# Using the second column half of one w_in block before its gate column exists, while the next block is still landing

## The chip, the cores and the metric

The kernel runs on one core of one Trainium2 chip. Times are device microseconds (us) of one execution. An execution is one sample; medians are given with their range and number. The effect looked for is about 0.1% of the time, smaller than the spread of single executions. Starts of instructions are in us from the start of the span.

## The reference, cut to what matters

The whole function mixes an attention branch and a gMLP branch with a gate. The part that is touched is the first product of the gMLP branch, and the gate's logit:

```python
z  = _gelu(jnp.einsum('bsd,df->bsf', x, w_in))     # x: 2048 x 512, w_in: 512 x 1376
z1 = z[..., :688]
z2 = _layernorm(z[..., 688:])
...
g  = _sigmoid((x * gate_w).sum(-1, keepdims=True)) # gate_w: 512
```

The kernel gets the logit almost for nothing: it stores gate_w as a 689th column beside the 688 columns of w_in that make z2.

## The kernel before

`w_z2` holds the z2 half of w_in in four blocks of 128 rows (the contraction, 512, in steps of 128). Each block has 688 columns from memory and the gate column at index 688. The columns are multiplied in two halves: half 0 is 344 columns, half 1 is 344 columns and the gate, 345. `xT` holds x transposed, in tiles of 128 rows of x.

```python
def z_one(zp, tt, wt, w, dt, j, first=0):          # one matmul: x tile tt, block dt, half j
    n = HF if j == 0 else w - HF                   # HF = 344
    nc.tensor.matmul(
        zp[:, j, 0:n], lhsT=xT[:, dt, tt * P:(tt + 1) * P],
        rhs=wt[:, dt, j * HF:j * HF + n],
        start=(dt == first), stop=(dt == NDT - 1),
    )

def gate_T():                                      # gate_w row -> column 688 of all four blocks
    gt = pq_tile([P, NDT])
    nc.tensor.matmul(gt[:, :], lhsT=gaterow[:, :], rhs=ident[:, 0:NDT], start=True, stop=True)
    nc.vector.tensor_copy(out=w_z2[:, :, FH], in_=gt[:, :])
```

The loads are issued so: half 0 of block 0, then blocks 1, 2 and 3 on one queue; two x tiles, half 1 of block 0, and the other x tiles on another; the gate row on a third. The first two x tiles are worked off in an order that follows the landings:

```python
def z2_first_two():
    # ... warm_up(n, w): n matmuls of constants, to get TensorE to its full clock;
    # ... one(tt, dt, j): z_one for x tile tt, with first=j
    warm_up(6); warm_up(2, P)
    # ... PE transposes of x tiles 0 and 1, mixed with one(0, 0, 0) and one(0, 1, 0) ...
    one(1, 0, 0)
    one(1, 1, 0)
    gate_T()
    one(0, 2, 0)                # block 2, half 0: here TensorE waits for block 2
    one(1, 2, 0)
    for dt in range(1, 3):      # blocks 1 and 2, half 1, with the gate column
        one(0, dt, 1)
        one(1, dt, 1)
    for tt in range(2):
        one(tt, 3, 0)
        one(tt, 0, 1)
        one(tt, 3, 1)
        z2_out(tt, zps[tt])
# then z2_tile(2), z2_tile(3), and so on: 8 matmuls each
```

The softmax here doesn't subtract the row's maximum and nothing guards it: scores larger than these inputs give would overflow.

Of the kernel before, what the change touches and what calls it, by code (L numbers as in the profile page):

```python
# [14 lines left out]
P = 128  # L15
# [6 lines left out]
HF = FH // 2  # L22
NT = S // P
NDT = D // P
# [11 lines left out]
def kernel(  # L36
# [14 lines left out]
    nc = tc.nc  # L51
# [10 lines left out]
    xT = pers.tile([P, NDT, S], BF16, name="xT")  # L62
    w_z1 = early.tile([P, NDT, FH], BF16, name="w_z1")
    w_z2 = early.tile([P, NDT, WP], BF16, name="w_z2")
# [111 lines left out]
    def next_turn(kind, n):  # L176
        turn[kind] += 1
        return f"{kind}{(turn[kind] - 1) % n}"

    def zp_tile():  # L180
        return psA.tile([P, 2, CH], FP32, name="zp", tag=next_turn("zp", 3))

    def pq_tile(shape, dtype=FP32):
        return psF.tile(shape, dtype, name="pq", tag=next_turn("pq", 2))

    def z_one(zp, tt, wt, w, dt, j, first=0):
        n = HF if j == 0 else w - HF
        nc.tensor.matmul(  # L188
            zp[:, j, 0:n], lhsT=xT[:, dt, tt * P:(tt + 1) * P],
            rhs=wt[:, dt, j * HF:j * HF + n],  # L190
            start=(dt == first), stop=(dt == NDT - 1),
        )

    def z_mm(tt, wt, w):
        zp = zp_tile()
        for dt in range(NDT):
            for j in range(2):
                z_one(zp, tt, wt, w, dt, j)
        return zp

    def z2_out(tt, zp):
        z2v = z2all[:, tt, :].rearrange("p (j n) -> p j n", j=2)
        nc.scalar.activation(out=z2v, in_=zp[:, :, 0:HF], func=AF.Gelu_apprx_tanh)  # L203
        nc.vector.tensor_copy(out=glog[:, tt:tt + 1], in_=zp[:, 1, HF:HF + 1])
        for j in range(2):
            nc.vector.bn_stats(out=bn6[:, tt, j, :], in_=z2v[:, j, :])  # L206
        nc.vector.bn_aggr(out=mv[:, tt, :], in_=bn6[:, tt, :, :].rearrange("p j s -> p (j s)"))
# [4 lines left out]
    def z2_first_two():  # L212
        zps = [zp_tile() for _ in range(2)]
        tp1 = psA.tile([P, 2, P], BF16, name="tp1", tag=next_turn("zp", 3))
        turn["zp"] -= 1

        def warm_up(n, w=CH):
            for _ in range(n):
                nc.tensor.matmul(
                    zps[0][:, 1, 0:w], lhsT=nc.const_aps.tensor(1.0, [P, P], BF16),  # L220
                    rhs=nc.const_aps.tensor(1.0, [P, w], BF16), start=True, stop=True)

        def one(tt, dt, j):
            z_one(zps[tt], tt, w_z2, FH + 1, dt, j, first=j)

        warm_up(6)
        warm_up(2, P)
        x_T(0, 0, 1, pq_tile([P, 1, P], BF16)[:, :, :])
        x_T(0, 1, NDT, pq_tile([P, 3, P], BF16)[:, :, :])
        warm_up(3, P)  # L230
        one(0, 0, 0)
        x_T(1, 0, 2, tp1[:, :, :])
        x_T(1, 2, NDT, pq_tile([P, 2, P], BF16)[:, :, :], on_act=True)
        one(0, 1, 0)
        warm_up(1, P)
        one(1, 0, 0)
        one(1, 1, 0)
        gate_T()
        one(0, 2, 0)
        one(1, 2, 0)  # L240
        for dt in range(1, 3):
            one(0, dt, 1)
            one(1, dt, 1)
        for tt in range(2):
            one(tt, 3, 0)
            one(tt, 0, 1)
            one(tt, 3, 1)
            z2_out(tt, zps[tt])
# [21 lines left out]
    def x_T(i, d0, d1, tp, on_act=False):  # L270
        for dt in range(d0, d1):
            nc.tensor.transpose(tp[:, dt - d0, :], xs[:, i, dt * P:(dt + 1) * P], ident[:, :])
        dst = xT[:, d0:d1, i * P:(i + 1) * P]
        if on_act:
            nc.scalar.copy(out=dst, in_=tp)
        else:
            with tc.high_priority():
                nc.vector.tensor_copy(out=dst, in_=tp)

    def gate_T():  # L280
# [3 lines that stand above are left out]
# [27 lines left out]
    with tc.manual_schedule(engines={mybir.EngineType.PE, mybir.EngineType.Activation}):  # L311
        z2_first_two()
        z2_tile(2)
        z2_tile(3)
        for c in range(NCH):
            ts = list(range(c * 4, c * 4 + 4))
            for tt in ts:
                if c > 0:
                    z2_tile(tt)
                if c >= 2 and tt % 4 == 1:  # L320
                    later = fold(3 - c)
            for tt in ts:
                z1_tile(tt)
                if c >= 2 and tt % 2 == 0:
                    later.pop(0)()
            z2_norm(ts)
            if c == 1:
                b_T()
# [268 lines left out]
```

## Time and profile before

| | before |
|---|---|
| time, median of 3 | 207.93 us (207.68 to 208.12) |
| span of the profiled execution | 206.3 us |
| TensorE (PE) busy | 202.2 us, 98% |
| TensorE waiting for block 2 | 0.2 us |

The busy table of the page, and the first line of its chain that ended last (shares of the span by engine):

```profile
PE 202.2 (98%) x1536; PEld 120.3 (58%) x1536; DVE 128.8 (62%) x276; ACT 76.5 (37%) x123; POOL 45.4 (22%) x73
...
PE 95%; DMA 2%; ACT 1%; ACTq 0%; DVE 0%; issue 0%
```

TensorE bounds the kernel. Its list of waits (us in total, times, longest) holds two entries in the whole execution:

```profile
PE zp L219 <- PEq L581: 0.8, 1, 0.8
PE zp L188 <- DMA w_z<-in_B_w_in_dram: 0.2, 1, 0.2
```

The second is the one in question. TensorE's timeline around it (start, duration, engine, line, instruction, count, in brackets the idle time before; the window asked for ends at 9.6 us). L188 is `z_one`, L219 the warm-up, L282 the matmul of `gate_T`:

```profile
5.32 0.31 PE L219 MATMUL zp<-const-bfloat16-1.0 128*128 128x128 bf16 x1
5.43 0.69 PE L188 MATMUL zp<-w_z,xT 128*128 128x344 bf16 x2
6.00 0.18 PE L282 MATMUL pq<-ident,gaterow 128*128 128x4 bf16 x1
6.41 3.38 PE L188 MATMUL zp<-w_z,xT 128*128 128x344 bf16 x22 [0.23 <-DMA w_z<-in_B_w_in_dram]
```

And the start of the chain in order of time: the load of block 2 lands at 1.74 + 4.62 us (6.37 before these are rounded), and the first matmul on it follows.

```profile
1.74 4.62 DMA w_z<-in_B_w_in_dram
6.37 0.04 issue
6.41 15.65 PE zp L188 x106
```

Two readings matter. First, one matmul's record is 0.31 us long, but matmuls overlap; what counts is the distance of their starts. For 344 columns that is 0.286 us before 5.90 us (as between the two of the second line) and 0.146 us after it: the clock doubled at 5.90 us in this execution. Second, TensorE really has room between about 6.0 and 6.4 us, more than the 0.23 us that the list shows, because the modelled end of the matmul before covers part of it.

The mark used from here on is the **stretch**: from the start of the first matmul on block 2 (6.409 us here) to the start of the first matmul of x tile 2 (8.163 us), 1.754 us. It is twelve matmuls, 12 x 0.146.

### The profile page before, as it was taken

The numbers are of one execution on the slowest core, as the hardware profiler recorded it, in microseconds if no ns is written. First come the engines' busy times: TensorE is split into PE (matmuls) and PEld (weight loads), VectorE is DVE, ScalarE is ACT, GpSimd is POOL, SyncE is SP. The second block draws the span as 40 slices with busy tenths as digits, with TensorE's granted clock in tenths as the row PEclk, the third lists the DMA queues.
The fourth block names the chain that finished last, engine by engine and source line by source line (L and its number), as shares of the span: only waits on it lengthen the run. The fifth ranks groups of instructions, "written<-read, shape, count | busy, mean of one in ns | idle before, by whom it ended". The sixth has DMA issues, their size and how long they took to land.

```text
span 206.3 us, 3946 instructions
## 1 busy us (share of the span) xinstructions
PE 202.2 (98%) x1536; PEld 120.3 (58%) x1536; DVE 128.8 (62%) x276; ACT 76.5 (37%) x123; POOL 45.4 (22%) x73
## 2 busy tenths in 40 slices
PE   8999999999999999999999999999999999999994
PEld 4566666655666555556565666555455555665642
DVE  3367565746977777979797778555466553633330
ACT  2756677796222243333424032222251126001322
POOL 5020202020522326244242422222204220200000
PEclk9999999999999999999999999999999999999999
DMA  6999499999998025940443229763554767353642
GB/s 169 268 199 182 91 235 210 253 210 248 208 290 147 3 38 131 322 93 15 88 28 64 51 38 117 144 115 73 105 153 89 79 104 190 58 104 70 129 91 78
DMA packets 90099, 27.22 MB, mean 132 GB/s; under 512 B 84224, under 2 KB 90080, under 8 KB 90080
## 3 DMA queue, kind: packets, MB, share of 16 engines
q1 hardware_dynamic: 87168, 24.28, 62.0%
q10 hardware_dynamic: 2880, 2.68, 4.1%
q8 instruction: 12, 0.20, 0.4%
q14 instruction: 7, 0.06, 0.1%
q0 software_dynamic: 32, 0.00, 0.0%
HBM read 4.15 MB, written 2.10 MB: 30 GB/s over the span
## 4 chain that ended last, share of the span: by engine, by line
PE 95%; DMA 2%; ACT 1%; ACTq 0%; DVE 0%; issue 0%
PE mm L441 36%; PE zp L188 17%; PE mm L346 14%; PE mm L480 8%; PE mm L478 7%; PE mm L386 7%; DMA w_z<-in_B_w_in_dram 2%; PE at L454 2%; PE kvacc L402 2%; PE mm L483 1%; PE zp L299 0%; ACT z1all L252 0%; ACT wq_p L306 0%; ACTq L117 0%; ACTq L120 0%; PE pq L299 0%
## 5 line engine op out<-in xcount | busy, mean ns | idle before, releaser
L441 PE MATMUL mm<-z2all,wspT 128*128 128x344 bf16 x512 | 79.9, 309 | 0.0
L441 PEld LDWEIGHTS <-wspT 128*128 128x128 bf16 x512 | 49.0, 98 | 25.7 <-issue 0.4
L188 PE MATMUL zp<-w_z,xT 128*128 128x344 bf16 (+1 forms) x256 | 38.9, 312 | 0.2 <-DMA w_z<-in_B_w_in_dram 0.2
L350 ACT ACTIVATE eq<-mm 128x512 bf16<-128x512 f32 x32 | 17.4, 594 | 51.3 <-PE mm L346 21.3
L354 DVE TENSOR_REDUCE zs<-eq 128x64 f32<-128x1024 bf16 x16 | 19.5, 1220 | 20.3 <-ACT eq L350 20.3
L188 PEld LDWEIGHTS <-xT 128*128 128x128 bf16 x256 | 24.9, 98 | 12.4 <-issue 0.3
L446 DVE SCALAR_TENSOR_TENSOR ucat<-mm,bT,z1all 128x344 bf16<-128x344 f32 x32 | 17.4, 544 | 21.9 <-PE mm L441 21.9
L363 POOL TENSOR_TENSOR eq<-eq,ratio 128x512 bf16<-128x512 bf16 x16 | 16.9, 1059 | 49.9 <-DVE ratio L362 41.7
L350 ACT ACTIVATE ek<-mm 128x512 bf16<-128x512 f32 x32 | 17.3, 600 | 27.4 <-PE mm L346 27.4
L494 ACT ACTIVATE ob<-mm,g_inv 128x512 bf16<-128x512 f32 (+1 forms) x16 | 10.9, 681 | 32.8 <-PE mm L483 28.3
L354 DVE TENSOR_REDUCE zs<-ek 128x64 f32<-128x1024 bf16 x16 | 19.3, 1210 | 2.8 <-ACT ek L350 2.8
L480 PE MATMUL mm<-wspT,uT 128*128 128x512 bf16 (+2 forms) x85 | 20.1, 366 | 0.0
L346 PEld LDWEIGHTS <-xT 128*128 128x128 bf16 x128 | 12.2, 98 | 13.2 <-PE mm L483 0.8
L363 POOL TENSOR_TENSOR ek<-ek,ratio 128x512 bf16<-128x512 bf16 x16 | 17.0, 1059 | 2.1 <-DVE ratio L362 1.5
L478 PE MATMUL mm<-wspT,oT 128*128 128x512 bf16 (+2 forms) x68 | 16.6, 366 | 0.0
L346 PE MATMUL mm<-wq_p,xT 128*128 128x512 bf16 x64 | 16.4, 379 | 0.0
L386 PE MATMUL mm<-wv_sb,xT 128*128 128x512 bf16 x64 | 16.4, 379 | 0.0
L346 PE MATMUL mm<-wk_p,xT 128*128 128x512 bf16 x64 | 16.3, 379 | 0.1
L206 DVE BATCH_NORM_STATS2 bn<-z2all 128x6 f32<-128x344 bf16 x32 | 14.9, 503 | 0.0
L203 ACT ACTIVATE z2all<-zp 128x688 bf16<-128x688 f32 x16 | 11.8, 744 | 6.3 <-PE zp L188 6.3
L252 ACT ACTIVATE z1all<-zp 128x688 bf16<-128x688 f32 x16 | 11.9, 744 | 5.1 <-PE zp L188 4.6
L480 PEld LDWEIGHTS <-uT 128*128 128x128 bf16 x85 | 8.1, 98 | 9.2
(72 smaller groups left out, 142.7 us busy)
## 6 DMA issues: line engine op xcount, KB each, us to landing
out_dram<-ob ACTq DMA_DIRECT2D x15, 128.0 KB, 1.7
wspT<-in_B_w_out_dram SPq DMA_DIRECT2D x2, 640.0 KB, 5.2
w_z<-in_B_w_in_dram SPq DMA_DIRECT2D x2, 344.0 KB, 5.2
w_z<-in_B_w_in_dram ACTq DMA_DIRECT2D x3, 172.0 KB, 4.6
wv_sb<-in_A_wqkv_dram SPq DMA_DIRECT2D x2, 256.0 KB, 3.5
wspT<-in_A_wo_dram SPq DMA_DIRECT2D x2, 256.0 KB, 3.9
xs<-in_A_x_dram SPq DMA_DIRECT2D x2, 128.0 KB, 2.7
uT<-ucat SPq DMA_TRANSPOSE x16, 2.8
```

The costliest lines, as they stand in the source:

```text
L188: nc.tensor.matmul(zp[:, j, 0:n], lhsT=xT[:, dt, tt * P:(tt + 1) * P], rhs=wt[:, dt, j * HF:j * HF + n], start=(dt == first), stop=(dt == ...
L206: nc.vector.bn_stats(out=bn6[:, tt, j, :], in_=z2v[:, j, :])
L252: nc.scalar.activation(out=z1all[:, tt, :].rearrange("p (j n) -> p j n", j=2), in_=zp[:, :, 0:HF], func=AF.Gelu_apprx_tanh,)
L346: nc.tensor.matmul(ps[:, :], lhsT=xT[:, dt, tt * P:(tt + 1) * P], rhs=w[:, dt, :], start=(dt == 0), stop=(dt == NDT - 1))
L350: nc.scalar.activation(out=e[:, :, a, :], in_=ps[:, :].rearrange("p (h f) -> p h f", f=DH), func=AF.Exp, scale=1.0 - 2.0 * a)
L354: nc.vector.tensor_reduce(out=z[:].rearrange("p h a -> p (h a)"), in_=e[:].rearrange("p h a f -> p (h a) f"), axis=AX.X, op=ALU.add,)
L363: nc.gpsimd.tensor_tensor(out=e[:, :, 1, :], in0=e[:, :, 1, :], in1=ratio[:, :, None].to_broadcast([P, H, DH]), op=ALU.mult)
L386: nc.tensor.matmul(v_ps[:, :], lhsT=xT[:, dt, tt * P:(tt + 1) * P], rhs=wv_sb[:, dt, :], start=(dt == 0), stop=(dt == NDT - 1))
L441: nc.tensor.matmul(gp[:, 0:HF], lhsT=wspT[:, st, tt * P:(tt + 1) * P], rhs=z2all[:, st, j * HF:(j + 1) * HF], start=(st == 0), stop=(st == ...
L446: nc.vector.scalar_tensor_tensor(out=ucat[tt % NU][:, c0 + j * HF:c0 + (j + 1) * HF], in0=gp[:, 0:HF], scalar=bT[:, tt:tt + 1], in1=z1all[ ...
L478: nc.tensor.matmul(acc, lhsT=oT[:, g, :], rhs=wo_t[:, g, c0:c1], start=(g == 0), stop=False)
L480: nc.tensor.matmul(acc, lhsT=uT[:, i + ft, :], rhs=w_main[i][:, ft, c0:c1], start=False, stop=False)
```

## The change

Half 1 of block 1 landed at 4.34 us, well before block 2. It is not used there because its last column is the gate, which comes from `gate_T`. The change uses its 344 weight columns at once, in the wait, and adds the gate column of that block later, by two matmuls of one column.

```diff
-            start=(dt == first), stop=(dt == NDT - 1),
+            start=(dt == first), stop=(dt == NDT - 1), skip_group_check=first > 0,
@@
+        def z_part(tt, dt, c0, c1, start):
+            nc.tensor.matmul(
+                zps[tt][:, 1, c0:c1], lhsT=xT[:, dt, tt * P:(tt + 1) * P],
+                rhs=w_z2[:, dt, HF + c0:HF + c1], start=start, stop=False, skip_group_check=True)
@@
         one(1, 0, 0)
         one(1, 1, 0)
+        for tt in range(2):
+            z_part(tt, 1, 0, HF, True)
         gate_T()
         one(0, 2, 0)
         one(1, 2, 0)
-        for dt in range(1, 3):
-            one(0, dt, 1)
-            one(1, dt, 1)
+        for tt in range(2):
+            one(tt, 2, 1)
+            z_part(tt, 1, HF, HF + 1, False)
```

Why the gate column may be written first by `one(tt, 2, 1)`, which does not set `start`: the Trainium skill, "PSUM — Partial Sum Buffer" (The four PSUM rules), says that a matmul with the start flag clears the written-bits of the whole 2 KiB bank, and that a later one without the flag overwrites where the bit is clear. The argument `skip_group_check` belongs to the language that the kernel is written in.

## The prediction

> **What bounds the kernel now.** TensorE: busy 202.2 of 206.3 us (busy table), 95% of the chain of waits. Its list of waits holds two entries: 0.8 us at the start, and 0.2 us for a block of w_in. The change aims at the second. In the timeline the last matmuls before it start at 5.43 and 5.71 us, the gate transpose (gate_T) at 6.00 (its row landed at 5.95), the next matmul at 6.41, because block 2 of w_in lands at 6.37. From there TensorE streams: 94 matmuls of 344 or 345 columns in 13.9 us, starts 146 ns apart.
>
> **What the change does.** The second column half of block 1 (landed at 4.34) needs the gate only in its last column. The other 344 columns are now multiplied before gate_T, and the gate column later by two one-column matmuls.
> - Out of the stream after 6.41: two 345-column matmuls, 292 ns.
> - Into it: two one-column matmuls with weight loads. The trace has none; the 128x68 matmuls of kvacc, each with its weight load, start 30 ns apart. The Trainium skill ("TensorE: Matmul & The Clock Gate", Back-to-back issue gap) gives about 25 ns as floor for 1 to 64 columns. Estimate 28 each, 56 in sum.
> - Into the wait: two 344-column matmuls. Matmuls of 344 columns start 286 ns apart before about 5.90 and 146 after: the clock doubles there. So these start at about 5.95 and 6.10, gate_T at about 6.24, and TensorE is free by 6.28, before block 2.
>
> Expected gain: 292 - 56 = about 0.24 us, all on the critical path: no later wait in TensorE's list can swallow it.
>
> **What can eat part of it.** Three margins shrink to nearly nothing:
> 1. The gate column's copy on VectorE starts 0.21 us after gate_T and takes 0.18: it ends at about 6.64 (now 6.39); its first reader comes at about 6.70.
> 2. Block 3 lands at 7.01 and is first read at 7.29 now; then at about 7.05.
> 3. x tiles 2 and 3 land at 7.88 and are first read at 8.16 now; then at about 7.93.
> So with these landings the gain cannot exceed about 0.24 us, and later landings cut it. Where the clock doubles later (the same page, on the clock gate, says its window runs free of the kernel's start), the two early matmuls take 286 ns each and gate_T goes past 6.41; I estimate a gain of 0.1 to 0.3 then. I expect 0.2 on the mean.
>
> **Predicted time.** 207.93 - 0.21 = 207.72 us, range 207.4 to 208.0. Three runs of before spread over 0.44 us, twice the gain. Chances: faster by over 2% 0.003, within 2% 0.994, slower 0.003.
>
> **What would show each step right or wrong.**
> - TensorE's timeline: two more 344-column matmuls between 5.7 and 6.3, gate_T at about 6.25, the wait for block 2 nearly gone, the first block-2 matmul still at about 6.41.
> - The one-column matmuls at about 6.85 and 7.02, each followed by the next within 30 ns. If they cost 60 to 100 each, the gain halves.
> - Block 3's first matmul at about 7.05, at most a short new wait; x tile 2's first at about 7.93.
> - The rest shifted by about 0.2 us.
>
> **What would make it wrong.** The gate copy becoming what is waited for; weight loads that do not hide behind a one-column matmul; block 3 or the x tiles landing as the next limit.

## The result, and the profile after

| | before | after |
|---|---|---|
| median | 208.00 us (207.68 to 208.12, 4 runs) | 207.72 us (207.41 to 208.26, 4 runs) |
| ratio | | 0.9992, interval 0.9967 to 1.0016 |
| first matmul on block 2 | 6.409 us | 6.558 us |
| first matmul of x tile 2 | 8.163 us | 8.068 us |
| stretch | 1.754 us | 1.510 us |
| span | 206.26 us | 206.14 us |

Ratios are the mean time of one kernel's fast runs over that of the other's of the same rounds, so not quite the ratio of the medians. The interval includes 1 by a wide margin: the times alone show no difference. The outputs are right.

The page after, busy table and chain. TensorE's busy time should not be compared: this trace has 1538 weight loads but 1520 matmul records, so 18 are missing.

```profile
PE 200.9 (97%) x1520; PEld 120.3 (58%) x1538; DVE 128.8 (62%) x276; ACT 76.5 (37%) x123; POOL 45.4 (22%) x73
...
PE 94%; DMA 2%; ACT 1%; issue 1%; ACTq 0%; DVE 0%
```

TensorE's waits after, the same two entries:

```profile
PE zp L219 <- PEq L588: 0.8, 1, 0.8
PE zp L188 <- DMA w_z<-in_B_w_in_dram: 0.4, 1, 0.4
```

TensorE's timeline after. L227 is `z_part`, L289 the matmul of `gate_T`:

```profile
5.41 0.47 PE L188 MATMUL zp<-w_z,xT 128*128 128x344 bf16 x2
5.71 0.46 PE L227 MATMUL zp<-w_z,xT 128*128 128x344 bf16 x2
6.00 0.17 PE L289 MATMUL pq<-ident,gaterow 128*128 128x4 bf16 x1
6.56 0.60 PE L188 MATMUL zp<-w_z,xT 128*128 128x344 bf16 x3 [0.39 <-DMA w_z<-in_B_w_in_dram]
6.99 0.17 PE L227 MATMUL zp<-w_z,xT 128*128 128x1 bf16 x1
7.02 0.31 PE L188 MATMUL zp<-w_z,xT 128*128 128x345 bf16 x1
7.17 0.16 PE L227 MATMUL zp<-w_z,xT 128*128 128x1 bf16 x1
7.19 2.65 PE L188 MATMUL zp<-w_z,xT 128*128 128x344 bf16 x17
```

The chain, where block 2 lands at 1.75 + 4.77 = 6.52 us:

```profile
1.75 4.77 DMA w_z<-in_B_w_in_dram
6.52 0.04 issue
6.56 0.60 PE zp L188 x3
```

The two early matmuls stand at 5.71 and 5.86 us. The one-column matmuls start at 6.994 and 7.167 us, and the next matmuls 27 and 26 ns behind them. The stretch is 0.244 us shorter, as worked out beforehand. But block 2 landed 0.148 us later in this execution, and the clock had doubled a whole us earlier (at 4.90 us). So only 0.095 us of the gain is left at x tile 2, and those 0.1 us then travel through the whole execution: TensorE's last matmul starts at 203.20 us before and 203.10 after.

Two questions remain. Was the later landing a cost of the change, or chance? And does every execution gain 0.244 us in the stretch?

### The profile page after: what moved, and what is told of

It is laid out like the page before. It is cut to its first block, busy times and chain, and to the rows that moved or that the text cites. A ratio compares the mean times of both kernels' runs of the same rounds, so it can differ in the third digit from the quotient of the medians.

```text
span 206.1 us, 3932 instructions
## 1 busy us (share of the span) xinstructions
PE 200.9 (97%) x1520; PEld 120.3 (58%) x1538; DVE 128.8 (62%) x276; ACT 76.5 (37%) x123; POOL 45.4 (22%) x73
## 4 chain that ended last, share of the span: by engine, by line
PE 94%; DMA 2%; ACT 1%; issue 1%; ACTq 0%; DVE 0%
PE mm L448 36%; PE zp L188 17%; PE mm L353 13%; PE mm L487 8%; PE mm L393 7%; PE mm L485 7%; DMA w_z<-in_B_w_in_dram 2%; PE at L461 2%; PE kvacc L409 2%; PE mm L490 1%; PE zp L306 0%; ACT z1all L259 0%; ACT wq_p L313 0%; ACTq L117 0%; ACTq L120 0%
## 5 line engine op out<-in xcount | busy, mean ns | idle before, releaser
L188 PE MATMUL zp<-w_z,xT 128*128 128x344 bf16 (+1 forms) x254 | 38.4, 310 | 0.5 <-DMA w_z<-in_B_w_in_dram 0.4
L485 PE MATMUL mm<-wspT,oT 128*128 128x512 bf16 (+2 forms) x62 | 15.6, 365 | 0.3
```

The costliest lines, as they stand in the source:

```text
L188: nc.tensor.matmul(zp[:, j, 0:n], lhsT=xT[:, dt, tt * P:(tt + 1) * P], rhs=wt[:, dt, j * HF:j * HF + n], start=(dt == first), stop=(dt == ...
L485: nc.tensor.matmul(acc, lhsT=oT[:, g, :], rhs=wo_t[:, g, c0:c1], start=(g == 0), stop=False)
```

## The experiments

The theory at first: the gain is TensorE work moved out of the stretch (two matmuls out, two of one column in), the landing is chance. Rivals: the change makes block 2 land later; or a landing, not TensorE's work, sets the length of the stretch; or the stretch is shorter for another reason than the filled wait.

### The kernel before, again (no edit)

> The kernel before, unchanged, timed against itself: it shows how far five rounds differ by chance. Every theory expects 1.000, within 0.15%. Its trace gives a second look at the same program: the stretch from the first matmul of block 2 to the first matmul of x tile 2 should again be 1.75 us (1.754 in the first trace), whatever block 2's landing; block 2 should land between 6.3 and 6.6 us.

Measured: 208.01 us (207.33 to 208.48, 6 runs) against itself, ratio 1.0008, interval 0.9993 to 1.0023. Five rounds (repeated executions of both) thus cannot tell 0.1%. Stretch 1.754 us, with block 2 landing at 6.58 us.

### The changed kernel, again (no edit)

> The changed kernel, unchanged. My theory (two 345-column matmuls leave the stretch behind block 2 and two one-column matmuls of 27 ns come in) expects that stretch to be 1.51 us again, 0.24 us below the kernel before, and a time 0.1 to 0.3 us lower: ratio 0.9985 to 0.9995. Rival: block 2 landed 0.15 us later in the first trace of the changed kernel because of the change, so that the gain is partly paid back there; then it lands at 6.5 or later again, while the repeat of the kernel before lands at 6.4 or earlier. Rival: the landing is chance; then the two repeats show no such order.

Measured: 208.00 us (207.50 to 208.51, 6 runs), ratio 1.0010, interval 0.9996 to 1.0024, on the same chip and rounds as the run above; the expected 0.9985 to 0.9995 lies below this interval, but the kernel before against itself gave 1.0008 in these rounds. Block 2 landed at 5.84 us, much earlier than in the two traces of the kernel before up to then, so the rival that the change delays it has no support. The stretch missed the expectation: 1.654 us, not 1.51. These are three lines of the timeline of all engines around it (CAST on DVE is the copy of the gate column into w_z2):

```profile
6.03 0.74 PE L188 MATMUL zp<-w_z,xT 128*128 128x344 bf16 x3
6.18 0.10 PEld L188 LDWEIGHTS <-xT 128*128 128x128 bf16 x1
6.24 0.17 DVE L290 CAST w_z<-pq 128x4 bf16<-128x4 f32 x1 [0.89 <-PE pq L289]
```

Three matmuls took 0.60 us in the first trace of the changed kernel; here they take 0.74. The third, `one(0, 2, 1)`, is the first to read the gate column. It started at 6.467 us, 53 ns after the copy ended at 6.414, and 0.144 us later than TensorE alone would have. Block 2 had landed before `gate_T` ran (6.005 us), so there was no wait left in which the gate's round trip could hide: TensorE to VectorE and back took 6.467 - 6.005 = 0.462 us. TensorE's list of waits does not show this 0.144 us, since the modelled end of the matmul before covers it.

### Only x tile 0 is split

```diff
-        for tt in range(2):
-            z_part(tt, 1, 0, HF, True)
+        z_part(0, 1, 0, HF, True)
@@
-        for tt in range(2):
-            one(tt, 2, 1)
-            z_part(tt, 1, HF, HF + 1, False)
+        one(0, 2, 1)
+        z_part(0, 1, HF, HF + 1, False)
+        one(1, 1, 1)
+        one(1, 2, 1)
```

> Only x tile 0 uses the split; x tile 1 has its 345-column matmul after block 2 as before. My theory expects half of the effect: the stretch from the first matmul of block 2 to the first of x tile 2 is 1.754 - 0.12 = 1.63 us, with one one-column matmul of 27 ns. If a landing (block 3 or x tile 2) and not TensorE's own work set the 1.51 us of the changed kernel, this stretch would be nearer to 1.51 than to 1.63.

Measured: 207.90 us (one run), stretch 1.776 us: a miss of 0.146. In this execution the clock doubled only at 6.23 us, so the early matmul was slow, `gate_T` started at 6.287 us, and block 2 (landed at 6.06) followed at once, at 6.316. The gate copy ended at 6.699, and the third matmul started at 6.751, 0.290 us behind the second instead of 0.145. Without that wait the stretch would be 1.776 - 0.145 = 1.63 us. That fits half of the effect, but only with the wait taken off by argument, so this run alone decides nothing.

### Half 1 of block 0 as well

```diff
+        for tt in range(2):                       # behind gate_T
+            z_part(tt, 0, 0, HF, False)
@@
             z_part(tt, 1, HF, HF + 1, False)
+            z_part(tt, 0, HF, HF + 1, False)
@@
             one(tt, 3, 0)
-            one(tt, 0, 1)
             one(tt, 3, 1)
```

> The same idea once more: the second half of block 0 (landed at 6.13 and 6.21 us in the two traces) is also used without its gate column in what is left of the wait, two more 344-column matmuls before block 2 and two more one-column matmuls behind it. If TensorE's work alone set the stretch, it would shrink by another 0.24 us to 1.27 us. I expect that the landing of x tiles 2 and 3 (7.81 and 7.88 us) stops it: with block 2's first matmul at 6.41 to 6.56, x tile 2's first matmul comes at 7.85 to 7.95 and waits for that landing by 0 to 0.2 us. Time: 0.1 to 0.3 us below the changed kernel, ratio to the kernel before 0.997 to 0.999.

Measured: 207.80 us (207.49 to 207.91, 5 runs), ratio 0.9998, interval 0.9986 to 1.0010. The stretch is 1.268 us, the value for TensorE's work alone; the x tiles landed at 7.41 and stopped nothing, against my expectation. The ratio is above the 0.997 to 0.999 expected. In the traced execution the four early matmuls (L227) did not fit ahead of block 2: the clock doubled late, at 6.47 us, block 2 landed at 5.94, and TensorE came to it only at 6.843. What the stretch gained there, the time ahead of it lost; the other four executions were not traced.

```profile
6.52 0.17 PE L291 MATMUL pq<-ident,gaterow 128*128 128x4 bf16 x1
6.55 0.45 PE L227 MATMUL zp<-w_z,xT 128*128 128x344 bf16 x2
6.84 0.60 PE L188 MATMUL zp<-w_z,xT 128*128 128x344 bf16 x3
```

### Block 2 made late: blocks 2 and 3 exchanged in the queue

Two kernels, the one before and the changed one, each with this edit:

```diff
-    load_z2w(nc.scalar, 2)
+    load_z2w(nc.scalar, 3)
     nc.sync.dma_start(out=w_z2[:, 0, HF:FH], in_=w_in_v[:, 0, FH + HF:F])
-    load_z2w(nc.scalar, 3)
+    load_z2w(nc.scalar, 2)
```

> The kernel before with blocks 2 and 3 of w_in loaded in the other order, so that block 2 lands where block 3 did (6.45 to 7.05 us so far) or later and block 3 is early. TensorE then waits long for block 2, whatever the clock and the gate row do. Every theory: the stretch from block 2's first matmul to x tile 2's is 1.75 us.

> The changed kernel with the same exchange. Theory now: a late block 2 is the case in which the change pays in full; the gate copy is long done (it ended at 6.42 us in two executions) and block 3 is there, so the stretch is 1.51 us. If the 1.65 us that the second execution of the changed kernel showed came from anything but the gate copy and the landings, it can show up here too.

Measured: 208.67 us before, 208.27 changed (one run each). TensorE's timeline, before and changed:

```profile
5.76 0.17 PE L282 MATMUL pq<-ident,gaterow 128*128 128x4 bf16 x1
7.12 2.35 PE L188 MATMUL zp<-w_z,xT 128*128 128x344 bf16 x15 [1.19 <-DMA w_z<-in_B_w_in_dram]
```

```profile
6.01 0.17 PE L289 MATMUL pq<-ident,gaterow 128*128 128x4 bf16 x1
6.94 0.60 PE L188 MATMUL zp<-w_z,xT 128*128 128x344 bf16 x3 [0.77 <-DMA w_z<-in_B_w_in_dram]
```

The stretch is 1.753 us (7.119 to 8.872) and 1.511 us (6.943 to 8.454). With a long wait the change pays its 0.242 us in full. The starts of x tile 2 differ by 0.418 us: 0.242 from the stretch, and 0.176 because block 2 happened to land that much earlier in the second execution.

### Block 2 never waited for: five more warm-up matmuls

Five 512-column warm-up matmuls are put in behind `one(1, 1, 0)`, so that TensorE comes late and everything has landed. In the kernel before:

```diff
         one(1, 1, 0)
+        warm_up(5)
         gate_T()
```

and in the changed kernel at the same place, ahead of its early matmuls:

```diff
         one(1, 1, 0)
+        warm_up(5)
         for tt in range(2):
             z_part(tt, 1, 0, HF, True)
         gate_T()
```

> The kernel before with five more 512-column warm-up matmuls right before the gate transpose, so that TensorE comes to block 2 about 1.1 us late and finds it landed. From the last warm-up to x tile 2's first matmul: 0.22 us (the warm-up) + 0.03 (gate transpose) + 1.75 + a wait of 0.14 us for the gate copy, whose first reader is now only 0.29 us behind block 2's first matmul: about 2.14 us.

> The changed kernel with the same five warm-ups, ahead of the early 344-column matmuls. There is no wait to fill, so my theory expects a loss: the two early matmuls cost what they save, and the two one-column matmuls add 2 x 27 ns. From the last warm-up to x tile 2's first matmul 2.14 + 0.05 = about 2.19 us. A rival by which the split itself shortens TensorE's work (for example by a shorter stretch behind block 2 whatever the wait) expects about 1.9 us.

TensorE's timeline, before and changed (L219 are the warm-ups, L283 and L290 the matmul of `gate_T`):

```profile
5.33 1.25 PE L219 MATMUL zp<-const-bfloat16-1.0 128*128 128x512 bf16 x5
6.42 0.17 PE L283 MATMUL pq<-ident,gaterow 128*128 128x4 bf16 x1
6.44 2.94 PE L188 MATMUL zp<-w_z,xT 128*128 128x344 bf16 x18
```

```profile
5.83 1.25 PE L219 MATMUL zp<-const-bfloat16-1.0 128*128 128x512 bf16 x5
6.93 0.45 PE L227 MATMUL zp<-w_z,xT 128*128 128x344 bf16 x2
7.22 0.17 PE L290 MATMUL pq<-ident,gaterow 128*128 128x4 bf16 x1
7.25 0.74 PE L188 MATMUL zp<-w_z,xT 128*128 128x344 bf16 x3
7.83 0.16 PE L227 MATMUL zp<-w_z,xT 128*128 128x1 bf16 x1
```

From the start of the last warm-up to x tile 2's first matmul: before 6.200 to 8.342, 2.142 us; changed 6.707 to 8.899, 2.192 us. Both numbers are as expected. Where there is no wait, the change costs 0.050 us, its two one-column matmuls. In both, the third matmul behind `gate_T` starts 0.46 us after it (6.417 to 6.880 and 7.217 to 7.681): the kernel before has the wait for the gate copy too, when nothing else is waited for. (The times, 208.14 and 208.70 us, one run each, are not comparable: the clock doubled at a different moment, so the warm-ups began at 5.33 and 5.83 us.)

### The gate transpose first

```diff
-        for tt in range(2):
-            z_part(tt, 1, 0, HF, True)
         gate_T()
+        for tt in range(2):
+            z_part(tt, 1, 0, HF, True)
```

> The changed kernel with the gate transpose moved ahead of the two early 344-column matmuls. In two traces of the split the third matmul behind block 2 started 0.14 us late, some 55 ns after the gate copy had ended; here the copy starts two matmuls (0.29 us at the full clock) earlier, unless the gate row lands late (it landed between 4.72 and 5.95 us). So the stretch from block 2's first matmul to x tile 2's should be 1.51 us in every execution, with an early block 2 too, where the changed kernel had 1.65. Rival: the 0.14 us are something else (a landing, the one-column matmuls); then it comes back here when block 2 lands early. Time: 0.1 to 0.25 us below the kernel before, ratio 0.9988 to 0.9995, which five rounds will hardly tell from 1.

Measured: 207.95 us (207.33 to 208.08, 6 runs), ratio 1.0003, interval 0.9990 to 1.0017. The stretch is 1.511 us, but this execution had a late block 2 (landed at 6.72 us), so it does not test the early case. The ratio lies above the 0.9988 to 0.9995 expected; the interval overlaps that range and includes 1.

### A third look at the kernel before (no edit)

> A third look at the kernel before. If it falls on an early block 2 (landing below 6.1 us), it shows what the kernel before does there: first matmul of block 2 within 0.05 us of that landing or of the gate transpose, and 1.754 us or more to x tile 2.

Measured: 207.78 us (one run). Block 2 landed at 5.97 us and its first matmul started at 6.070, 0.073 us behind `gate_T` at 5.997 (I had expected 0.05). The kernel before has early landings of block 2 as well. The stretch is 1.897 us, 0.143 more than 1.754:

```profile
6.07 0.74 PE L188 MATMUL zp<-w_z,xT 128*128 128x344 bf16 x3
6.28 0.18 DVE L283 CAST w_z<-pq 128x4 bf16<-128x4 f32 x1 [0.92 <-PE pq L282]
```

The first two of the three matmuls start 0.218 us apart, because the clock doubled at 6.26 us, during the first. The second and the third start 0.217 us apart, and that is not the clock: the second started at 6.288 and its record is 0.31 us long, as at the full clock. The third, the first reader of the gate column, started at 6.505, 53 ns after the gate copy had ended at 6.452, as in the changed kernel above. So the kernel before waited for the gate copy too, by 0.07 us, in an ordinary execution with an early block 2.

### The gate transpose first, and no wait

```diff
+        warm_up(5)
         gate_T()
         for tt in range(2):
             z_part(tt, 1, 0, HF, True)
```

> The gate-first order with the five extra warm-ups ahead of it, so that no landing is waited for. The two kernels measured in this condition took 2.142 us (before) and 2.192 us (changed) from the last warm-up to x tile 2's first matmul, both with a wait of 0.146 us ahead of the third matmul behind the gate transpose. If that wait is for the gate copy, it is gone here, because two more matmuls stand between the gate transpose and the copy's first reader: 2.192 - 0.146 = 2.046 us. If it is anything else about the third matmul behind block 2 (a landing, the PSUM bank), it stays: 2.19 us.

```profile
7.21 0.17 PE L290 MATMUL pq<-ident,gaterow 128*128 128x4 bf16 x1
7.24 0.45 PE L227 MATMUL zp<-w_z,xT 128*128 128x344 bf16 x2
7.44 0.17 DVE L291 CAST w_z<-pq 128x4 bf16<-128x4 f32 x1 [2.09 <-PE pq L290]
7.53 0.60 PE L188 MATMUL zp<-w_z,xT 128*128 128x344 bf16 x3
```

From the last warm-up to x tile 2: 6.993 to 9.040, 2.047 us; expected 2.046. The group of three takes 0.60 us again: the copy runs beside the early matmuls. So the 0.146 us were the wait for the gate copy, shown by taking away what made it. In this condition the gate-first order beats both kernels, by 0.095 and 0.145 us. (Its time, 208.88 us in one run, again says nothing: the warm-ups came even later.)

### A third look at the changed kernel (no edit)

> The changed kernel a third time, timed in five more rounds. The stretch from block 2's first matmul to x tile 2's should be 1.51 us if block 2's first matmul comes 0.15 us or more after the gate transpose, up to 1.65 us if it comes at once behind it. The time should follow x tile 2's first matmul: span = that start + 198.05 to 198.11 us, as in all twelve traces so far. Ratio to the kernel before: 0.998 to 1.001, not to be told from 1.

Measured: 207.80 us (207.48 to 208.09, 6 runs), ratio 0.9999, interval 0.9984 to 1.0015. The expectation on the stretch missed: block 2's first matmul came 0.18 us behind `gate_T` (6.291 and 6.110), so that 1.51 us was expected; there was no wait for the gate copy, and the stretch is still 1.650 us. Here it is block 3:

```profile
6.90 0.16 PE L227 MATMUL zp<-w_z,xT 128*128 128x1 bf16 x1
6.90 1.14 PEld L188 LDWEIGHTS <-xT 128*128 128x128 bf16 x8
7.07 1.18 PE L188 MATMUL zp<-w_z,xT 128*128 128x344 bf16 x7
```

The matmul behind the second one-column matmul is the first on block 3. It started 0.166 us behind it (6.900 to 7.066 us) instead of 0.026, 43 ns after block 3 had landed at 7.023. That is 0.14 us of the gain lost to the next landing. The cause is read from the time of the landing: the first matmul on block 2, where it was waited for, also starts 41 to 43 ns after its landing (six traces). No run takes this wait away on purpose. In the changed kernel with the blocks exchanged, where block 3 had long landed (6.269), the same distance was 0.026 us.

The span followed x tile 2 as expected: in all fourteen traces, whatever the kernel, the span is the start of x tile 2's first matmul plus 198.05 to 198.11 us.

## Why the prediction was right or wrong

**The size of the move: right.** Two matmuls out at 0.146 us, two of one column in at 26 to 28 ns: 0.244 us in the first trace, 0.242 in the pair with a late block 2. The Trainium skill ("TensorE: Matmul & The Clock Gate", Back-to-back issue gap) gives about 25 ns as the least distance of two starts; the traces agree: the one-column matmuls here, weight loads included, start 25 to 28 ns ahead of the next matmul where nothing is waited for.

**That no later wait swallows it: right.** Span minus x tile 2's start is constant within 0.06 us over fourteen traces. Whatever is gained or lost before 8 us arrives at the end.

**The median, 207.72 us: met, but not evidence for the gain.** The repeats of the changed kernel gave ratios of 1.0010 and 0.9999, and the kernel before against itself 1.0008. The 0.28 us between the first medians is within chance.

**The mean gain of 0.2 us: the term that was too large.** The prediction took block 2's landing, 6.37 us, as given. It landed between 5.84 and 6.58 us in the six traces of the two kernels unaltered. The step "with these landings the gain cannot exceed about 0.24 us, and later landings cut it" was made for the gate row, block 3 and the x tiles, and leaves out block 2. For block 2 the sign is the other: a late block 2 pays in full, an early one does not. What the three executions of the changed kernel gained can be estimated by laying the order of the kernel before onto their own landings (block 2's landing + 0.04 us, then 1.754 us):

| execution of the changed kernel | block 2 lands | x tile 2, kernel before (estimate) | x tile 2, measured | gain |
|---|---|---|---|---|
| first | 6.52 | 8.31 | 8.068 | 0.24 |
| second | 5.84 | 7.64 | 7.687 | -0.05 |
| third | 6.25 | 8.04 | 7.941 | 0.10 |

Their mean is about 0.1 us, half of the predicted 0.2. Three executions, with an estimate in one column, are too few to fix the mean. What they show is that single executions range from a small loss to the whole 0.24; that the mean is below 0.2 is likely, but not shown. In the second, TensorE came to block 2 after it had landed: no wait was left, the change added its one-column matmuls, and `gate_T` stood two matmuls later, so that the gate copy was waited for.

**The three margins: two of them showed.** The gate copy held the stream up by 0.144 us in the second execution, block 3 by 0.14 us in the third. Block 3 was not late there (7.02 us, against 7.01 and 7.05 in the first two traces); it became the next wait because block 2 had come earlier. The x tiles held nothing up. The prediction named all three but counted them as touching; with their own spread they bind in some executions.

**The clock: right in kind.** The prediction used the one moment of doubling that it saw, 5.90 us. It was 4.90 us in the first trace of the changed kernel, so `gate_T` stayed at 6.00 us instead of moving to 6.24. In none of the three traces of the changed kernel did it double after 5.90, so the prediction's estimate for that case, a gain of 0.1 to 0.3 us, was not tested.

**The wait for block 2 nearly gone: wrong in that trace.** It was 0.39 us, more than before (0.23), since block 2 came later and the early matmuls ran at the full clock.

Left open: whether the gate-first order is better than the kernel before in ordinary executions. It removes the wait for the gate copy, which the kernel before showed in one of its three traces (0.07 us), but it would hold up the early matmuls when the gate row lands late (it landed between 4.6 and 6.1 us), and its time (ratio 1.0003) cannot be told from 1. Also open is a small effect of the change on the landings themselves, which six traces do not exclude (block 2 at 5.97, 6.37 and 6.58 us before, at 5.84, 6.25 and 6.52 changed).

## What to carry to other kernels

Work moved into a wait is worth what leaves the stream behind it only in the executions in which that wait exists; look at several executions before taking one landing time as fixed, and ask what becomes the next thing to be waited for. When a producer with a round trip to another engine stands in TensorE's stream, try the new filler behind it, not ahead of it, unless the producer's own input may be late; here this saved 0.145 us where nothing else was waited for (2.192 to 2.047 us). For effects below the noise of the time, measure start to start between two fixed instructions, and make the condition certain (a late load, or a filled wait) rather than repeating runs.

## What the Trainium skill lacked or had wrong

- "TensorE: Matmul & The Clock Gate" (Part 1, What you observe) gives the moment at which the clock doubles as varying by 500 ns either way from run to run. In the twelve of fourteen traces that recorded it here, it lay between 4.90 and 6.52 us. In the other two (the kernel before with no wait, and the third look at the changed kernel) the starts of 128-column matmuls went from 107 to 56 ns apart by 3.9 and 3.7 us. TensorE's first matmul was always at 0.85 us, so the spread is over 2.5 us. So 500 ns is too narrow for this kernel; a note further down on the page, that one kernel shows 6, 11 or 14 slow matmuls from run to run, points the same way. That the window runs free of the kernel agrees.
- "Perfetto Trace Analysis" (Identifying the Most-Contended Engine) warns that matmul busy time is a poor measure of how near the limit a kernel is, because matmuls are pipelined. It does not say that waits are hidden the same way: the waits of 0.14 us, for the gate copy and for block 3, appear in no list of waits here. A 344-column matmul's record lasts 0.31 us while starts are 0.146 apart, and a one-column matmul's record 0.16 us while starts are 0.026 apart, so the record before covers the wait. They show only in the distance of starts, or in a group of three that lasts 0.74 us instead of 0.60.
- I found no figure in the pages for a round trip from a matmul over a small VectorE copy back to a matmul. Where it was waited for it took 0.46 us from start to start, in four executions here, and 0.51 us in a fifth whose clock doubled on the way (a 4-column matmul, a 128x4 copy out of PSUM of 0.18 us, the matmul that reads it).
- "DMA: Bandwidth & Descriptors" does not tell, as far as I saw, how much one load's landing varies between executions of one program. The 172 KB load of block 2, issued at 1.71 to 1.75 us each time, took 4.1 to 4.8 us in six executions of the two kernels.
